# Attention in front of two dense layers: where a tile's values stand, who transposes the last tile, and how much filling a late step gets

## The chip, the cores and the metric

One core of a Trainium2 chip runs the kernel. The metric is device time in microseconds (us); lower is better. PE is TensorE, DVE VectorE, ACT ScalarE, POOL GpSimd, and SP the engine whose queue issues most DMAs.

## The reference

Batch 2, 8 heads, 768 positions, head dimension 64. Each position attends to the first 8 positions and to the last 96, with a bias that falls with distance; then two dense layers follow, a mixture of four experts and a SoLU layer.

```python
scores = scale * np.matmul(q, k.transpose(0, 1, 3, 2)) + bias
scores = np.where(keep, scores, -1e9)
a = softmax(scores)
attn = np.matmul(a, v)                       # x: 1536 tokens of 512
for e in range(E):                           # 4 experts, hidden 1024
    out += p[:, e:e + 1] * (np.maximum(x @ w1[e], 0.0) @ w2[e])
h = out @ w_in                               # SoLU layer, LayerNorm, then
return layernorm(h * softmax(h)) * g_ln @ w_out
```

## The kernel before, in words

The 1536 queries stand in 12 tiles of 128. A unit is one tile and one pair of heads, so unit u belongs to tile u // 4, and there are 48. The first 14 units are worked one by one. From then on the loop at line 1571 takes steps t = 14, 16, ..., 50 and starts two units in each. A pair of units passes through these stages, each in a later step:

- Step t: `scores` (L1223), two PE products per unit into one PSUM tile, `sps`. In `soft_pair` DVE then adds the bias and finds the maximum (L1274), and ACT takes the exponential (L1281).
- Step t+2: `soft_pair` normalizes the pair (sum L1260, reciprocal L1261, product L1265 on POOL or DVE). Then the probabilities are transposed, in one of two ways. The plain way is `stage_b`: eight PE transposes (L1305) and two ACT copies into `pts` (L1307). The other is `turn`: two DVE block transposes (L1317), a DMA store, and in step t+4 four DMA loads into `pts_turned` (`turned_back`, L1324). `turned(u)` says which it is: the first two units of the tiles in `TURNED`.
- The values, `stage_c` (L1350): sixteen PE products per pair into the PSUM tile `x`. A plain pair has them at the end of step t+4, a turned pair at the front of step t+8. After the last pair of a tile, ACT copies `x` into `xh` (L1363) and DVE subtracts the rest into `xl` (L1364). There is one `x` tile, so the next tile's first values need L1364 done. The turned pair of a tile is its last one.

Between these stages the loop calls `pull(share)`, twice in most steps. It issues pieces of the first expert's products, three PE matmuls each (L552 or L583, 256 wide for the first 512 tokens, 512 wide for the next), until their cost (320 or 640) has used up the share. An overrun or a rest is carried to the next pull. A pull also ends where the next block of tokens isn't ready, which drops the rest, and between the two products of a block of tokens 512 wide, which keeps it (`yield 0, None`, L848). What no pull has issued runs after the loop, in `rest_of_moe`; the last block of 512 tokens always does, since it needs all of attention.

The share of a step is 2 x 312, from step 36 on 2 x 750, plus half of (1970 - other), where `other` counts the step's transposes and values. The order of instructions on every engine is the order of the program (`manual_schedule`).

On the trace, step 24 begins with the scores at 55.84 us, step 26 at 61.89, step 32 at 76.14, 34 at 82.19, 36 at 86.26, 42 at 104.33, 44 at 111.33 and 46 at 117.99. Steps 48 and 50 have no scores: their first values begin at 124.35 and their last at 129.82, and the last block of the first expert starts at 132.32.

Of the kernel before, what the change touches and what calls it, by code (L numbers as in the profile page):

```python
# [34 lines left out]
EARLY = 312  # L35
# [11 lines left out]
HALF = 512  # L47
PAIRS = 14
FORMS = 36
TURNED = 4, 6, 8, 9, 10, 11  # L50


@with_exitstack
def kernel(ctx, tc, ep, qk, vp, nn, pr, wall, w64, gl, out):
# [1093 lines left out]
    def fast_arm():  # L1148
        st = stream("f")
        with ExitStack() as es:  # L1150
# [24 lines left out]
            st_p, st_rs, st_pt, st_x = {}, {}, {}, {}  # L1175
            NU = 4 * NSLOT
            NAT = 2
            N0 = 4 * NAT

            def unit(u):  # L1180

                return (u % 2, u // 2) if u < N0 else divmod(u, 4)
# [11 lines left out]
            def load_v(s):  # L1194
                if s < NSLOT:
                    v = vpl.tile([128, 2, 512], F32, tag="v", name="v")
                    nc.sync.dma_start(out=v, in_=vp[s])
                    vts[s] = v

            def geom(s):  # L1200

                if SLOTS[s][1] == 0:
                    return 1, None, (1,)
                if KEY_OF[s] % RING == 0:
                    return 2, 128, (1, 0)
                return 2, 0, (0, 1)

            def scores(u):

                s, pr_ = unit(u)  # L1210
                pos = KEY_OF[s] % RING
                out_ = sps[:, :, u % 2]
                for a in range(2):
                    r = slice(64 * a, 64 * a + 64)
                    if geom(s)[0] == 1:
                        nc.tensor.matmul(out_[:, a, 0:128], lhsT=qs[s][r, pr_], rhs=kr[r, pr_, pos, 32:160],
                                         start=True, stop=True)
                    else:

                        k = kr[r, pr_, 0, 0:128]  # L1220
                        c0, d = (32, 160 * (RING - 1) - 32) if pos == 0 else (160 * (pos - 1), 192)
                        rhs = bass.AP(tensor=k.tensor, offset=k.offset + c0, ap=[list(k.ap[0]), [d, 2], [1, 128]])
                        nc.tensor.matmul(out_[:, a], lhsT=qs[s][r, pr_], rhs=rhs, start=True, stop=True)  # L1223
# [86 lines left out]
            def turned(u):  # L1310

                return u % 4 < 2 and u // 4 in TURNED

            def turn(u0):
                for u in (u0, u0 + 1):
                    p, k = st_p.pop(u), 4 * (u % 2)
                    nc.vector.transpose(out=blocks.rearrange("p (jj c q) -> p c jj q", jj=4, c=8)[:, k:k + 4],  # L1317
                                        in_=p.rearrange("p a (c jj f) -> p (a c) jj f", c=2, jj=4))
                nc.sync.dma_start(out=t_dram[u0 // 4 % 2], in_=blocks)
# [10 lines left out]
            def stage_c(u, hold=None):  # L1330
                s, pr_ = unit(u)
                nch, _, parts = geom(s)
                t = st_pt.pop(u)
                if u < N0:
                    x, place = x0[:, 2 * (pr_ % 2):2 * (pr_ % 2) + 2], s
                else:
                    if s not in st_x:
                        st_x[s] = psX.tile([128, 4, 128], F32, tag="x", name="x")
                    x, place = st_x[s], pr_
                for c in range(nch):  # L1340
                    for a in range(2):
                        h = 2 * pr_ + a
                        if s < NAT:
                            v = v0[:, s, 64 * h:64 * h + 64]
                        else:
                            v = vts[s][:, parts[c], 64 * h:64 * h + 64]
                        to, r = x[64 * a:64 * a + 64, place], t[nch * a + c]
                        if turned(u):
                            to = to.rearrange("p (i q) -> p i q", i=4)
                        nc.tensor.matmul(to, lhsT=v, rhs=r,  # L1350
                                         start=(c == 0), stop=(c == nch - 1))
                if u < N0 and s == NAT - 1:
                    xc = slice(pr_, pr_ + 1), slice(0, 128 * NAT)
                elif u >= N0 and pr_ == (1 if turned(u) else 3) and not turned(u - 2):
                    xc = slice(0, 4), slice(128 * s, 128 * s + 128)
                else:
                    return
                h_, l_ = xh[:, xc[0], xc[1]], xl[:, xc[0], xc[1]]
                if u < N0:
                    x = x.rearrange("p s c -> p (s c)").unsqueeze(1)  # L1360

                def evict():
                    nc.scalar.copy(h_, x)  # L1363
                    late.append(lambda: nc.vector.tensor_tensor(out=l_, in0=x, in1=h_.bitcast(F32), op=ALU.subtract))  # L1364

                if hold is None:
                    evict()
                else:
                    hold.append(evict)
# [74 lines left out]
            def next_operands(s, pr_):  # L1444

                if pr_ == 0:
                    for j in LOAD_AFTER.get(s - 1, ()):
                        load_keys(j, copies)
                    if s > 3:
                        load_q(s + 1)  # L1450
# [70 lines left out]
            for t in range(N0, PAIRS):  # L1521
                s, pr_ = divmod(t, 4)
                share = SHARE.get(t, EARLY if t < N0 + 12 else 400 if t < N0 + 27 else 750)
# [46 lines left out]
                    st.load_piece()  # L1570
            for t in range(PAIRS, NU + 3, 2):

                other = 870 * (not turned(t - 2)) + 1100 * (not turned(t - 4)) + 1100 * turned(t - 8)
                share = 2 * (EARLY if t < N0 + 27 else 750) + (1970 - other) // 2
                hold, landed = [], copies[:]
                del copies[:]
                if t < NU:
                    for u in (t, t + 1):
                        scores(u)
                if turned(t - 8) and t <= NU:  # L1580
                    for u in (t - 8, t - 7):
                        stage_c(u, hold)
                if t < NU:
                    for u in (t, t + 1):
                        next_operands(*divmod(u, 4))
                if turned(t - 4):
                    turned_back(t - 4)
                if turned(t - 8):
                    load_v((t - 8) // 4 + 2)
                soft_pair(t)  # L1590
                for f in landed:
                    f()
                while late:
                    late.pop()()
                while st.rests:
                    st.rests.pop(0)()
                for f in hold:
                    f()
                if turned(t - 2):
                    turn(t - 2)  # L1600
                if t <= NU:
                    st.behind = False
                    pull(share)
                for _ in range(2):
                    next(rest_p, None)
                if t <= NU and not turned(t - 2):
                    for u in (t - 2, t - 1):
                        stage_b(u)
                if t < NU:
                    tokens[0] = 128 * done  # L1610
                    st.behind = t < NU - 2
                    if t > PAIRS:
                        pull(share)
                while late:
                    late.pop()()
                if not turned(t - 4):
                    for u in (t - 4, t - 3):
                        if u in st_pt:
                            stage_c(u)
                if t > NU and turned(t - 6):  # L1620
                    pull(share)
                    for u in (t - 6, t - 5):
                        stage_c(u)
                if t % 4 == 2 and not turned(t - 6):
                    done = (t - 2) // 4
                    load_v(done + 1)
                elif turned(t - 8):
                    done = (t - 4) // 4
                if t == FORMS:
                    st.forms = st.x_forms(lambda: [st.rawp.tile([128, 512], F32, tag="raw", name="fraw")  # L1630
                                                   for k in range(2)])
                if st.forms and t < NU:
                    for f in st.forms.pop(0):
                        f()
                if t < NU:
                    for u in (t, t + 1):
                        st.split_piece("act" if u < N0 + 12 and u % 2 else "dve", "pool")
                        st.load_piece()
# [180 lines left out]
```

## Time and profile before

| What | Value |
|---|---|
| Median of 3 runs | 725.35 us (725.05 to 726.32) |
| Profiled execution | 723.35 us, its span 721.6 us |
| PE busy | 705.5 us, 98% of the span |
| DVE, POOL, ACT busy | 498.5, 350.6, 301.2 us |
| Chain that ended last | PE 92%, DVE 3%, ACT 2%, DMA 1%, issue 1% |
| Granted TensorE clock | 1.000 of full speed |

Busy shares are means over stages with different limits. A row of the timeline has the start, the duration, the engine, line and operation, and in brackets how long the engine had been idle and what released it. Ends of matmuls are modelled and overlap the next start, so the time that PE loses at a wait is read from starts to starts.

### The profile page before, as it was taken

To read this page: it belongs to the slowest core of one execution; us is meant where nothing else is said; L and a number is where in the kernel's file an instruction comes from. 1 tells how busy PE (TensorE), PEld (TensorE's weight loads), DVE (VectorE), ACT (ScalarE), POOL (GpSimd) and SP (SyncE) were. 2 spreads that over 40 slices of the span, in tenths; PEclk is the share of its full clock that TensorE was granted. 3 is DMA by queue.
4 is the path that set the end of the run, shared out by engine and by line. 5 is a ranking of instruction groups with operands and counts; after the bars stand their busy time and mean duration, and the time that the engine had idled before them with its cause. 6 is when DMAs were issued, how large, how long until landed. Compare 5 with 4: busy or idle time off the path is not lost.

```text
span 721.6 us, 11067 instructions
## 1 busy us (share of the span) xinstructions
PE 705.5 (98%) x3815; PEld 586.5 (81%) x3815; DVE 498.5 (69%) x1088; ACT 301.2 (42%) x676; POOL 350.6 (49%) x407
## 2 busy tenths in 40 slices
PE   8999899899999999999999999999999999999997
PEld 5787777688889889888888988888898888888886
DVE  6776656647785685677568568857965667778870
ACT  5876654422533333242333325324434324454452
POOL 6733476466694156218216522630735089555600
PEclk9999999999999999999999999999999999999999
DMA  8655563420342324234132423423332690333341
GB/s 252 149 170 160 155 175 118 146 74 15 118 134 86 102 89 117 62 101 131 59 107 84 132 73 110 123 69 97 99 103 73 249 362 1 120 115 124 111 129 50
DMA packets 59921, 85.61 MB, mean 119 GB/s; under 512 B 6224, under 2 KB 37200, under 8 KB 59856
## 3 DMA queue, kind: packets, MB, share of 16 engines
q1 hardware_dynamic: 59296, 84.39, 37.3%
q8 instruction: 32, 0.52, 0.3%
q10 hardware_dynamic: 560, 0.43, 0.2%
q14 instruction: 33, 0.27, 0.1%
HBM read 62.75 MB, written 22.04 MB: 118 GB/s over the span
## 4 chain that ended last, share of the span: by engine, by line
PE 92%; DVE 3%; ACT 2%; DMA 1%; issue 1%; SPq 0%; POOL 0%; DVEq 0%; POOLq 0%; ACTq 0%
PE fg L583 36%; PE fg L760 18%; PE fo L1088 9%; PE fh L989 8%; PE fg L675 7%; PE fg L552 5%; PE x L1350 3%; PE sps L1223 3%; PE pt L1305 1%; PE g L1377 1%; PE wp L134 1%; DVE fg L688 1%; DVE p L1274 1%; DMA v<-in_vp_dram 1%; ACT fhh L644 1%
## 5 line engine op out<-in xcount | busy, mean ns | idle before, releaser
L583 PE MATMUL fg<-fhh,wV 128*128 128x512 f32 (+1 forms) x800 | 242.0, 383 | 0.3
L583 PEld LDWEIGHTS fg<-fhh,wV 128*128 128x128 f32 x800 | 147.9, 188 | 32.9 <-issue 2.5
L583 PE MATMUL fg<-fhl,wV 128*128 128x512 f32 (+1 forms) x400 | 149.2, 381 | 0.3 <-DVE fhl L567 0.2
L583 PEld LDWEIGHTS fg<-fhl,wV 128*128 128x128 f32 x400 | 74.9, 188 | 15.3 <-DVE fhl L567 0.8
L309 POOL TENSOR_TENSOR wR<-kr,wR 128x512 fp32r<-128x512 f32 (+1 forms) x28 | 29.1, 1060 | 96.4 <-ACT wR L301 96.3
L644 ACT ACTIVATE fhh<-fg 128x512 fp32r<-128x512 f32 x80 | 47.5, 598 | 66.6 <-DVE fg L770 40.3
L602 POOL TENSOR_TENSOR scr<-scr,kr 128x512 f32<-128x512 f32 x24 | 31.0, 1293 | 61.5 <-DVE kr L601 61.5
L645 DVE SCALAR_TENSOR_TENSOR fhl<-fg,fhh 128x512 fp32r<-128x512 f32 x80 | 54.1, 686 | 7.0 <-ACT fhh L644 5.4
L760 PE MATMUL fg<-xt,fwS 128*128 128x512 f32 x252 | 58.3, 389 | 0.0
L760 PEld LDWEIGHTS fg<-xt,fwS 128*128 128x128 f32 x252 | 47.3, 188 | 9.8
L760 PE MATMUL fg<-xh,wR 128*128 128x512 f32 x168 | 54.0, 389 | 0.0
L770 DVE TENSOR_TENSOR fg<-kr,fg 128x512 f32<-128x512 f32 x42 | 29.0, 694 | 33.4 <-PE fg L760 23.0
L597 DVE TENSOR_TENSOR fg<-fg,pb 128x512 f32<-128x512 f32 x59 | 40.9, 693 | 14.6 <-PE fg L583 14.2
L1265 POOL TENSOR_TENSOR p<-p,su 128x512 f32<-128x512 f32 x24 | 28.0, 1179 | 45.3 <-DVE su L1261 30.9
L1281 ACT ACTIVATE p<-p,mn 128x256 f32<-128x256 f32 x68 | 33.9, 499 | 28.8 <-DVE mn L1274 27.7
L598 DVE TENSOR_TENSOR scr<-fg,scr 128x512 f32<-128x512 f32 x59 | 40.8, 692 | 2.0
L552 PE MATMUL fg<-xh,wR 128*128 128x512 f32 (+1 forms) x128 | 38.6, 372 | 1.4 <-DVE xl L1364 1.4
L760 PEld LDWEIGHTS fg<-xh,wR 128*128 128x128 f32 x168 | 31.5, 188 | 6.6
L309 POOL TENSOR_TENSOR fwS<-kr,fwS 128x512 fp32r<-128x512 f32 x28 | 35.8, 1299 | 2.2 <-ACT fwS L301 2.2
L1274 DVE CUSTOM_DVE_ANT_0 p<-sps,btab 128x256 f32<-128x256 f32 x68 | 25.0, 420 | 15.7 <-PE sps L1223 15.6
L1088 PE MATMUL fo<-xt,fhh 128*128 128x512 f32 (+1 forms) x156 | 35.4, 375 | 0.0
L765 ACT COPY kr<-fg 128x512 f32<-128x512 f32 x42 | 24.2, 590 | 25.6 <-PE fg L760 25.6
(286 smaller groups left out, 1501.7 us busy)
## 6 DMA issues: line engine op xcount, KB each, us to landing
w_dram<-fr SPq DMA_DIRECT2D x44, 256.0 KB, 2.5
kr<-in_wall_dram SPq DMA_DIRECT2D x42, 256.0 KB, 2.9
fr<-in_w_dram SPq DMA_DIRECT2D x32, 256.0 KB, 2.7
pb<-p_dram SPq DMA_DIRECT2D x22, 256.0 KB, 3.3
v<-in_vp_dram SPq DMA_DIRECT2D x10, 512.0 KB, 4.0
kr<-t_dram SPq DMA_DIRECT2D x32, 128.0 KB, 2.9
frawt<-in_wall_dram SPq DMA_DIRECT2D x14, 256.0 KB, 2.8
t_dram<-tmp SPq DMA_DIRECT2D x6, 512.0 KB, 3.0
```

Of the source, the lines that this page charges most:

```text
L309: e.tensor_tensor(out=w[:, 1], in0=t, in1=w[:, 0].bitcast(F32), op=ALU.subtract)
L552: nc.tensor.matmul(ps[:, :n], lhsT=w[:, a, k], rhs=b[:, k, cols], start=(k == 0 and i == 0), stop=(k == 3 and i == 2))
L583: nc.tensor.matmul(ps[:, :n], lhsT=w[:, a, k], rhs=b[k], start=(i == 0), stop=(i == 11))
L597: nc.vector.tensor_tensor(out=ps[:, :n], in0=ps[:, :n], in1=pg, op=ALU.mult)
L598: nc.vector.tensor_tensor(out=a, in0=ps[:, :n], in1=a, op=ALU.add)
L644: nc.scalar.activation(th, src, AF.Relu)
L645: residuals.append(lambda: nc.vector.scalar_tensor_tensor(out=tl, in0=src, scalar=0.0, in1=th.bitcast(F32), op0=ALU.max, op1=ALU.subtract))
L675: nc.tensor.matmul(ps[:, q_ * q:q_ * q + q_], lhsT=w[:, a, j], rhs=x[b][j], start=(opens and q == j == m == 0), stop=(j == 1 and m == 2), ...
L760: nc.tensor.matmul(ps, lhsT=w[:, a, j], rhs=x[b][j], start=(i in (1, 2, 5) and j == 0 and m == 0), stop=(j == 1 and m == 2), skip_group_ch ...
L989: nc.tensor.matmul(ps[i], lhsT=left[i][x][j], rhs=right[i][j][:, y], start=(i in (1, 5, 2) and j == m == 0), stop=(j == 1 and m == 2), ski ...
L1088: nc.tensor.matmul(ps, lhsT=a[:, fc % 4], rhs=wo[fc][:, i % 2, c0:c0 + n], start=(fc == i == 0), stop=(fc == 7 and i == 2))
L1281: nc.scalar.activation(p[:, a], p[:, a], AF.Exp, bias=mn[:, a:a + 1], scale=-1.0, accum_out=st_rs[u][:, a, 0:1])
```

## The change

The last tile, 11, is no longer turned. Where the tile before has a turned pair, the values of the next tile's first two units move from step t+4 to step t+6, where they stand together with those of its last two units. The share from step 36 on is 2 x 680 in place of 2 x 750, and `other` counts the values of a step as they now stand.

```diff
-TURNED = 4, 6, 8, 9, 10, 11
+TURNED = 4, 6, 8, 9, 10
+LATE = 680
...
+            def valued(t):
+
+                if turned(t - 4) or turned(t - 8) and t <= NU:
+                    return []
+                return list(range(t - 6 if turned(t - 10) and not turned(t - 6) else t - 4, t - 2))
...
-                other = 870 * (not turned(t - 2)) + 1100 * (not turned(t - 4)) + 1100 * turned(t - 8)
-                share = 2 * (EARLY if t < N0 + 27 else 750) + (1970 - other) // 2
+                other = 870 * (not turned(t - 2)) + 550 * len(valued(t)) + 1100 * turned(t - 8)
+                share = 2 * (EARLY if t < N0 + 27 else LATE) + (1970 - other) // 2
...
-                if not turned(t - 4):
-                    for u in (t - 4, t - 3):
-                        if u in st_pt:
-                            stage_c(u)
+                for u in valued(t):
+                    if u in st_pt:
+                        stage_c(u)
```

`valued` gives no units in steps 24 and 32 and four in steps 26 and 34; it gives units 44 to 47 in step 50. The branch for a turned pair at the end (`if t > NU and turned(t - 6)`), which had one more pull in step 50, is no longer taken.

## Rows read from the trace of the kernel before

**Rows 1.** part 1 of the page: busy time, share and instructions by engine.

```profile
PE 705.5 (98%) x3815; PEld 586.5 (81%) x3815; DVE 498.5 (69%) x1088; ACT 301.2 (42%) x676; POOL 350.6 (49%) x407
```

**Rows 2.** stretches: busy us (instructions) of PE, PEld, DVE, ACT, POOL; clock; DMA.

```profile
118.00:124.40 6.40, 6.40 (x45) 4.96 (x46) 6.11 (x20) 2.59 (x9) 4.62 (x4) 1.00 0.21 85
124.40:132.30 7.90, 4.97 (x63) 3.92 (x57) 3.57 (x6) 3.00 (x6) 0.41 (x1) 1.00 0.73 218
132.30:721.60 589.30, 583.97 (x2840) 493.12 (x2840) 410.30 (x736) 219.16 (x411) 280.88 (x324) 1.00 0.33 106
```

**Rows 3.** waits of PE from 30 to 135 us: total us, times, longest us.

```profile
PE x L1350 <- DVE xl L1364: 2.4, 2, 1.4
PE x L1350 <- DMA pts_turned<-t_dram: 1.4, 2, 1.0
PE fg L552 <- DVE xl L1364: 1.4, 1, 1.4
PE x L1350 <- ACT pts L1307: 0.6, 1, 0.6
```

**Rows 4.** timeline of PE, steps 24 and 26.

```profile
59.28 0.36 PE L552 MATMUL fg<-xh,wR 128*128 128x256 f32 x1
...
60.87 1.09 PE L1350 MATMUL x<-pts,v 128*64 128x128 f32 x16 [0.99 <-DVE xl L1364]
61.89 1.14 PE L1223 MATMUL sps<-kr,q 64*128 64x256 f32 x8
```

**Rows 5.** timeline of PE, steps 32 to 36.

```profile
78.69 1.03 PE L1305 MATMUL pt<-ident,p 128*128 128x128 f32 x8
81.17 1.09 PE L1350 MATMUL x<-pts,v 128*64 128x128 f32 x16 [1.45 <-DVE xl L1364]
82.19 1.14 PE L1223 MATMUL sps<-kr,q 64*128 64x256 f32 x8
83.26 0.39 PE L583 MATMUL fg<-fhh,wV 128*128 128x256 f32 x1
...
85.23 1.09 PE L1350 MATMUL x<-pts,v 128*64 128x128 f32 x16
...
87.87 0.63 PE L1305 MATMUL pt<-ident,p 128*128 128x128 f32 x4 [0.48 <-DVE p L1265]
88.68 0.66 PE L1305 MATMUL pt<-ident,p 128*128 128x128 f32 x4 [0.18 <-POOL p L1265]
```

**Rows 6.** timeline of PE, steps 44 and 46.

```profile
115.62 1.03 PE L1305 MATMUL pt<-ident,p 128*128 128x128 f32 x8
116.41 0.48 PE L583 MATMUL fg<-fhh,wV 128*128 128x512 f32 x1
...
117.99 1.14 PE L1223 MATMUL sps<-kr,q 64*128 64x256 f32 x8
```

**Rows 7.** timeline of PE, steps 48 and 50 and the block behind them.

```profile
126.14 1.04 PE L1305 MATMUL pt<-ident,p 128*128 128x128 f32 x8
127.73 1.09 PE L1350 MATMUL x<-pts,v 128*64 128x128 f32 x16 [0.55 <-ACT pts L1307]
129.82 1.09 PE L1350 MATMUL x<-pts_turned,v 128*64 128x128 f32 x16 [0.99 <-DMA pts_turned<-t_dram]
132.32 0.50 PE L552 MATMUL fg<-xh,wR 128*128 128x512 f32 x1 [1.41 <-DVE xl L1364]
```

**Rows 8.** timeline of DVE, steps 32, 34 and 48.

```profile
80.42 0.69 DVE L1364 TENSOR_TENSOR xl<-x,xh 128x512 fp32r<-128x512 f32 x1 [1.64 <-ACT xh L1363]
...
84.78 1.30 DVE L1317 STREAM_TRANSPOSE tmp<-p 128x512 f32<-128x512 f32 x2
...
126.95 0.68 DVE L1364 TENSOR_TENSOR xl<-x,xh 128x512 fp32r<-128x512 f32 x1
```

**Rows 9.** timeline of POOL, the normalizing products of steps 34 and 46.

```profile
81.56 2.04 POOL L1265 TENSOR_TENSOR p<-p,su 128x512 f32<-128x512 f32 x2 [4.21 <-DVE su L1261]
...
119.71 2.04 POOL L1265 TENSOR_TENSOR p<-p,su 128x512 f32<-128x512 f32 x2 [3.61 <-DVE su L1261]
```

## The prediction

> **What bounds the kernel now.** I read part 1 of the page first: PE is busy for 98% of the span [rows 1], so time can come only from the places where PE stands still or from work taken off PE. The stretches come next. Behind 132.30 us PE is busy for 583.97 of 589.30 us, while just before it 4.97 of 7.90 us are busy [rows 2]. The part behind 132.30 can therefore only be shifted as a whole: what attention gains in front of it reaches the end, and what it loses does too. Then the waits of PE inside attention: 2.4 us in two waits of the values for L1364, 1.4 us in two for the loads of the turned pairs, 1.4 us at the first product behind attention, 0.6 us for the copies of the transposes [rows 3]. The timeline of PE shows where they lie: step 24, step 32, and four places in steps 48 and 50 seen as three gaps [rows 4, 5, 7].
>
> Because the ends of matmuls are modelled, I measure each gap from starts to starts. Prices first. A piece of filling 256 wide: five of them run from 83.26 to 85.23, 0.39 us each [rows 5]. A run of two pieces 512 wide: 116.41 to 117.99, 1.58 us; eight PE transposes: 115.62 to 116.41, 0.79 us [rows 6]. Sixteen value products: 60.87 to 61.89, 1.02 us [rows 4]. Scores of a step: 82.19 to 83.26, 1.07 us [rows 5].
>
> **Part one: values stand together a step later.** In step 24 PE ends its one piece at 59.28 + 0.39 = 59.67 and starts the values at 60.87, so 1.20 us are lost [rows 4]. In step 32 the transposes end at 78.69 + 0.79 = 79.48 and the values start at 81.17: 1.69 us [rows 5]. Both gaps have one cause. The turned pair at the front of the step completes its tile, and the next tile's values need the single `x` tile, which DVE's L1364 gives back at 80.42 + 0.69 = 81.11 [rows 8], behind ACT's exponentials and copy. The change puts these values behind the next step's scores and filling, some 3 us later, when L1364 is long done. The work itself is kept: adding up shares and costs, steps 24 and 26 issue 1 + 6 pieces now and 4 + 3 then, steps 32 and 34 1 + 5 and 4 + 2.
>
> What is late next is the pair's chain through DVE and POOL. The next wait, at the transposes of step 36 (87.87 and 88.68), stays, since there PE already runs ahead of L1265 [rows 5]. But that chain starts from the scores of step 34, which move 1.69 us earlier, so the wait moves with it if nothing in between is tied to something that doesn't move. One thing is: POOL's products of step 34 follow DVE's sum behind L1364, and run from 81.56 to 83.60 whatever PE does [rows 9]. DVE's two block transposes read them, the first from 84.78 - 1.6 = 83.2, the second some 0.65 later at 83.85 [rows 8]. The second product is done 0.25 us before; the cover is thin. If it is gone, the cost is what POOL is late by; from below the cost is 0, from above the gain of this step, 1.69 us. I take 0. Part one: 1.20 + 1.69 = 2.89 us.
>
> **Part two: the last tile is transposed by PE.** It adds eight transposes, 0.79 us of PE [rows 6], and two ACT copies. ACT has 2.59 us of work in the 6.40 us of step 46 [rows 2], which covers them. It removes two block transposes on DVE, one store and four loads. In steps 48 and 50 the gaps of PE are: from 126.14 + 0.79 = 126.93 to 127.73, 0.80 us for the copies of pair 46; from 127.73 + 1.02 = 128.75 to 129.82, 1.07 us for the loads of pair 44; from 129.82 + 1.02 = 130.84 to 132.32, 1.48 us for the eviction of the last tile [rows 7]. Together 3.35 us. The second goes, as there are no loads. The first goes too: the values of pair 44, transposed two steps before, now stand ahead of those of pair 46, and 0.79 + 1.02 = 1.81 us pass from the start of the transposes to the values of 46, where 127.73 - 126.14 = 1.59 us were needed [rows 7]. Pair 44 needs L1364 of the tile before; it ends at 127.63 now, held by a piece in front of it in DVE's order [rows 8], and 1.5 us more filling stands ahead of the transposes then.
>
> A new wait can come in step 46, at the transposes of pair 44, which need POOL's products. In the old order these end at 119.71 + 2.04 = 121.75 [rows 9]; PE would be there at 117.99 + 1.07 for scores + 1.58 for two pieces = 120.64, so the wait lies between 0 and 1.1 us. I take 0: the sum in front of the products was late because DVE's queue waited for the fourth piece of a group in the second pull of step 44, and with the new shares that group ends in the first.
>
> The Trainium skill ("VectorE: DVE Perf Modes", section on the three transpose paths) gives 390 ns for a 128x128 transpose on TensorE and 311 ns for VectorE's blocks. By its price the eight would cost an estimated 3.12 us in place of 0.79 and the whole gain would be about 3.0 us; the trace has them starting 0.1 us apart, and I hold to the trace.
>
> **Part three: smaller late shares.** They remove no work; they keep some for later. Added up from step 36 on, in pieces 512 wide: now 4, 6, 4, 6, 5, 6, 1, all 32 of the block, so nothing is left when the last tile is evicted. Then 3, 6, 4, 3, 7, 4, 3 = 30: two pieces are left, and no pull stands in step 50. They run behind the last values and before the last block, 1.58 us against the gap of 1.48 [rows 6, 7], so the third gap is covered. The second pull of step 42 issues nothing, as it meets the border between the two products; its credit goes to step 44. Step 42 is then short, 1.07 + three pieces + 1.02 us, some 4.3 us in all.
>
> **The sum.** 2.89 + 3.35 - 0.79 = 5.45 us; I take 5.3 for joints of 0.1 us. The profiled execution took 723.35 us, its span 721.6, and would come to 718.05. The median of the runs is 725.35, 2.0 us above the profiled one; I carry the same difference over: 725.35 - 5.3 = 720.1 us.
>
> **Rivals.**
> 1. The chain of one pair takes over: the waits of steps 24 and 32 go, but PE meets them again in step 36, since POOL's products of step 34 don't move [rows 9]. Against it: 0.25 us of cover. Gain 5.3 - 1.7 = 3.6 us, or 721.8 us.
> 2. The end doesn't pay: a new wait in step 46 (1.1 us) and two pieces that come too early or too late to cover the eviction (1.5 us). For it: the two pieces cross from one section of the program to the next, where buffers are laid out anew. Gain 5.3 - 2.6 = 2.7 us, or 722.7 us.
> 3. The change doesn't do what it says: the waits return at other places for nearly their whole length, because the steps run at the rate of DVE and POOL. Gain under 1.4 us, 724 to 726.8 us.
> 4. Slower: with fewer pieces in steps 36 to 46, PE falls to the rate of the chain from scores over DVE, ACT and POOL to the transposes, in each of six steps. DVE was busy for 6.11 of 6.40 us in step 46 [rows 2], which speaks for it; the two block transposes taken out there and the even filling of the other steps speak against. It decides from 5.3 / 6 = 0.9 us a step; at 1.2 us it costs 7.2 and gives 725.35 + 1.9 = 727.3 us.
>
> **How the numbers follow.** Forecast 0.58, rivals 0.15, 0.13, 0.08 and 0.06. Less than 0.2%, 1.45 us, can't be told from no change here. Faster by more: 0.58 + 0.15 + 0.13 = 0.86; same 0.08; slower 0.06. The range: at best the gaps go and the shorter runs of filling save some start costs, 6.7 us, 718.6; on the other side it takes in the first two rivals and the edge of the third, 723.9.
>
> **What would show it.** Right: no wait of L1350 for L1364; pair 20 and 28 behind the filling of steps 26 and 34; 136 transposes at L1305 and 80 value products from `pts_turned`; six L583 products between the last values and the first L552 of the last block, which starts without a wait; PE still waiting at the transposes of step 36 by about as much as now. Wrong: a wait of more than 0.5 us at L1305 in step 46, at L1223 in step 44, or a longer one in step 36; or idle time behind the last block's start, where I expect none new.

## The result: 7.65 us faster, where 5.3 were forecast

| | before | changed |
|---|---|---|
| Median of 4 runs | 725.84 us (725.05 to 726.98) | 718.19 us (717.23 to 718.84) |
| Profiled execution | 723.35 us, span 721.6 | 718.38 us, span 716.6 |
| Ratio | | 0.9892 (0.9874 to 0.9911) |

The forecast was 720.1 us in a range of 718.6 to 723.9. The measured 718.19 lies below it. The profiled execution, on the other hand, came to 718.38 where 718.05 was forecast. So what the forecast got wrong isn't in the difference of the two profiles; it is in what the runs of before have on top of their profile. The two profiles agree with the forecast in part by luck, as the end of this section shows.

First part 1 of the changed kernel's page (busy time, share of the span, instructions by engine), which answers to [rows 1]: PE is busy about as long as before, in a span that is 5.0 us shorter.

```profile
PE 706.1 (99%) x3823; PEld 587.7 (82%) x3823; DVE 497.8 (69%) x1086; ACT 302.1 (42%) x678; POOL 349.2 (49%) x407
```

Its waits of PE from 30 to 135 us (total, times, longest) answer to [rows 3]. L1357 is the old L1350, L1371 the old L1364, L1306 the old L1305. None of the waits for L1371 is left, neither of the values nor of the last block. One wait for a turned pair's loads remains.

```profile
PE x L1357 <- DMA pts_turned<-t_dram: 0.5, 1, 0.5
PE pt L1306 <- DVE mn L1275: 0.4, 1, 0.4
PE pt L1306 <- DVE p L1266: 0.3, 1, 0.3
PE pt L1306 <- POOL p L1266: 0.2, 1, 0.2
```

Its timeline of PE in steps 24 and 26 answers to [rows 4]: the scores of step 24 and the values of the turned pair, two pieces, the transposes, two pieces, the scores of step 26, and behind three more pieces 32 value products at once. No row has an idle time.

```profile
56.40 1.13 PE L1224 MATMUL sps<-kr,q 64*128 64x256 f32 x8
...
58.49 0.38 PE L553 MATMUL fg<-xh,wR 128*128 128x256 f32 x1
...
59.30 1.03 PE L1306 MATMUL pt<-ident,p 128*128 128x128 f32 x8
60.09 0.36 PE L553 MATMUL fg<-xh,wR 128*128 128x256 f32 x1
...
60.98 1.13 PE L1224 MATMUL sps<-kr,q 64*128 64x256 f32 x8
...
63.31 1.97 PE L1357 MATMUL x<-pts,v 128*64 128x128 f32 x32
```

Steps 32 to 36, for [rows 5]: the wait for the loads in step 32, the values of both pairs together, and the next wait, which stands where it stood, at the transposes of step 36, and came forward with everything else.

```profile
76.70 1.09 PE L1357 MATMUL x<-pts_turned,v 128*64 128x128 f32 x16 [0.50 <-DMA pts_turned<-t_dram]
...
82.19 1.97 PE L1357 MATMUL x<-pts,v 128*64 128x128 f32 x32
84.09 1.13 PE L1224 MATMUL sps<-kr,q 64*128 64x256 f32 x8
85.55 0.63 PE L1306 MATMUL pt<-ident,p 128*128 128x128 f32 x4 [0.33 <-DVE p L1266]
86.36 0.66 PE L1306 MATMUL pt<-ident,p 128*128 128x128 f32 x4 [0.18 <-POOL p L1266]
```

Steps 46 to 50, for [rows 6, 7]: the new transposes at 116.29, the last ones at 122.73, all values of the last tile at 123.69, two pieces at 125.59, and the last block at 127.07 without a wait. The two pieces are just enough: DVE's L1371, which that block needs, ends at 126.33 + 0.69 = 127.02.

```profile
116.29 1.03 PE L1306 MATMUL pt<-ident,p 128*128 128x128 f32 x8
...
122.73 1.04 PE L1306 MATMUL pt<-ident,p 128*128 128x128 f32 x8
123.69 1.97 PE L1357 MATMUL x<-pts,v 128*64 128x128 f32 x32
125.59 0.50 PE L584 MATMUL fg<-fhh,wV 128*128 128x512 f32 x1
...
127.07 0.50 PE L553 MATMUL fg<-xh,wR 128*128 128x512 f32 x1
```

```profile
126.33 0.69 DVE L1371 TENSOR_TENSOR xl<-x,xh 128x512 fp32r<-128x512 f32 x1 [3.51 <-ACT xh L1370]
```

From the scores of step 24 to the last block, PE takes 127.07 - 56.40 = 70.67 us, where it took 132.32 - 55.84 = 76.48 [rows 7]: 5.81 us less. What lies behind is no shorter, as the stretch that answers to [rows 2] shows (busy time of PE, weight loads, DVE, ACT, POOL; clock; DMA).

```profile
127.00:716.60 589.60, 584.19 (x2842) 493.09 (x2840) 411.44 (x738) 219.05 (x411) 280.24 (x324) 1.00 0.33 108
```

The spans differ by 5.0 us and not by 5.81, because step 24 begins 0.56 us later in this execution (56.40 for 55.84) and the part behind takes 0.3 us more. Nothing ahead of step 24 was changed; in the fourteen profiles of this case it begins anywhere from 55.80 to 57.08 us. So the forecast of 718.05 for the profiled execution came out within 0.33 us because a larger gain than the one summed up, 5.81 us for 5.45, came together with a later start.

### The profile page after: what moved, and what is told of

It reads as the page before. It is cut to its first block, busy times and chain, and to the rows that moved or that the text cites. A ratio compares the mean times of both kernels' runs of the same rounds, so it can differ in the third digit from the quotient of the medians.

```text
span 716.6 us, 11078 instructions
## 1 busy us (share of the span) xinstructions
PE 706.1 (99%) x3823; PEld 587.7 (82%) x3823; DVE 497.8 (69%) x1086; ACT 302.1 (42%) x678; POOL 349.2 (49%) x407
## 4 chain that ended last, share of the span: by engine, by line
PE 95%; DVE 1%; ACT 1%; SPq 1%; DMA 1%; issue 0%; POOL 0%; DVEq 0%
PE fg L584 37%; PE fg L761 19%; PE fo L1089 9%; PE fh L990 8%; PE fg L676 7%; PE fg L553 6%; PE x L1357 3%; PE sps L1224 2%; PE pt L1306 2%; PE g L1384 1%; PE wp L135 1%; DMA pts_turned<-t_dram 1%; DVE fg L689 1%; ACT fhh L645 1%; PE fh L1070 0%
```

## Experiments

The question was where the missing 2.35 us come from. Theory C: PE's gaps in steps 48 and 50 let the granted clock fall in most executions of the kernel before, though not in the profiled one. Rival S: the runs spread by chance at the start. The first four kernels also take the change apart.

**The kernel before against itself.**

> The kernel before, unchanged, timed against itself. The prediction carried the 2.0 us by which the runs of before lay above its profiled execution over to the changed kernel; there the profiled execution (718.38 us) lies among the runs (717.23 to 718.84). Theory S (start): the difference is chance at the start, where the granted clock rises at a time that varies; then this kernel's runs spread over 723 to 727 us at a granted clock of 0.998 to 1.000, and the profile loses or gains the time in the first 8 us. Rival C (clock behind the gaps): PE's gaps in steps 48 and 50 let the granted clock fall in some executions; then the runs at 725 to 727 us show 0.996 to 0.998, with the loss between 126 and 140 us, and a kernel without the gaps doesn't have them.

725.76 us, ratio 1.0006 (0.9991 to 1.0022). Its own profile has full clock throughout, but the runs, each listed with its mean granted clock, fall into groups. The 101 runs of the kernel before that were timed with these experiments:

| Mean granted clock | Runs | Median | Range |
|---|---|---|---|
| 0.999 and 1.000 | 25 | 723.57 us | 723.08 to 724.71 |
| 0.997 and 0.998 | 52 | 725.45 us | 723.16 to 726.16 |
| 0.996 and less | 24 | 726.84 us | 726.20 to 729.54 |

Where the clock is granted throughout, the kernel before takes about what its two profiles took, 723.35 and 723.52 us. About two runs in three lie above 724.7, nearly all with a lower mean clock. The size fits as well: a mean of 0.997 to 0.998 over 722 us is an estimated 1.4 to 2.2 us of lost clock, and the median of that group lies 1.9 us above the first. That fits C, but it doesn't show the place yet, and no profile of the kernel before caught a fall.

S is right about a smaller part. The first twelve products of PE take 4.38 to 5.49 us in the fourteen profiles, and the start of step 24 moves by 1.3 us; the 25 runs at full clock spread over 1.6 us.

**Part one alone** (`TURNED` with tile 11, `LATE = 750`).

```diff
-TURNED = 4, 6, 8, 9, 10
-LATE = 680
+TURNED = 4, 6, 8, 9, 10, 11
+LATE = 750
```

> Part one alone: the values behind a turned tile stand together a step later; the last tile stays turned and the late share stays 750. By the theory of the gaps PE loses 1.20 and 1.69 us less in steps 24 and 32 and the three gaps in steps 48 and 50 (3.35 us) stay: 2.9 us less than before, both in the runs and between the start of step 24 and the last block. By the rival that the chain through POOL takes the second gap back in step 36: 1.2 us. By C the runs stay above the profiled execution as those of before do.

721.60 us, ratio 0.9957 (0.9941 to 0.9972), 3.1 us less than before by that ratio. The four fastest runs, at full clock, lie at 720.57 to 720.80, 2.9 us under 723.5, as worked out; five of the twelve runs lie at 722.28 to 725.34, with 0.998 and less. This profile caught the clock falling. The rows are stretches of 2 us at the end of attention; the third column from the right is the granted clock (1.00 is 2.4 GHz, 0.50 is 1.2 GHz).

```profile
124.00:126.00 2.00, 1.45 (x14) 1.14 (x14) 1.30 (x3) 1.16 (x3) 0.00 (x0) 1.00 0.61 178
126.00:128.00 2.00, 1.02 (x18) 0.78 (x16) 0.00 (x0) 0.00 (x0) 0.00 (x0) 1.00 0.97 277
128.00:130.00 2.00, 0.96 (x16) 0.71 (x15) 0.38 (x1) 0.99 (x2) 0.00 (x0) 1.00 0.99 283
130.00:132.00 2.00, 1.63 (x5) 1.33 (x6) 2.00 (x4) 1.15 (x3) 0.94 (x1) 0.72 1.01 340
132.00:134.00 2.00, 2.00 (x7) 1.52 (x6) 2.00 (x2) 0.00 (x0) 1.92 (x2) 0.50 0.68 239
134.00:136.00 2.00, 2.00 (x10) 1.62 (x9) 1.86 (x2) 0.62 (x1) 1.37 (x2) 0.92 0.01 3
```

PE is busy for 1.45, 1.02 and 0.96 us of three stretches of 2 us; then, with PE busy again, the clock goes to half, and it is back in the last stretch. The part behind the start of the last block takes 720.9 - 130.37 = 590.5 us, 1.2 more than [rows 2]: that is about what this fall costs. The timeline of PE shows the same three gaps as [rows 7], and behind them two products that take 1.05 us at 132.24, where two take 0.63 in the kernel before (132.89).

```profile
125.79 1.09 PE L1357 MATMUL x<-pts,v 128*64 128x128 f32 x16 [0.56 <-ACT pts L1308]
127.86 1.09 PE L1357 MATMUL x<-pts_turned,v 128*64 128x128 f32 x16 [0.98 <-DMA pts_turned<-t_dram]
130.37 0.50 PE L553 MATMUL fg<-xh,wR 128*128 128x512 f32 x1 [1.41 <-DVE xl L1371]
...
132.24 1.05 PE L553 MATMUL fg<-xh,wR 128*128 128x512 f32 x2
```

**Part two alone** (the kernel before, with `TURNED = 4, 6, 8, 9, 10`).

> Part two alone: the last tile is transposed by TensorE, values where they stood before, late share 750. The wait for the loads (1.07 us) goes, eight transposes come (0.79 us), one piece of filling is left for the eviction (0.7 of 1.48 us). The values of units 44 and 45 now stand in step 48, behind those that complete the tile before, so by the theory of the gaps they wait for L1364 as in steps 24 and 32, 1.2 to 1.7 us: together 0.3 us faster to 0.7 us slower than before. By the rival that the loads were the costly part of the end: 2 us faster or more.

722.57 us, ratio 0.9958 (0.9943 to 0.9973), and all ten runs within 721.80 to 722.92 at a clock of 0.998 and above. From step 24 to the last block it takes 75.06 us, 1.4 less than before. Against the runs of before at full clock the median is 1.0 us lower; the rest of the 2.9 us below 725.47 is the clock of the runs of before, as no run of this kernel stands apart. My expectation was off: the values of pair 44 didn't wait for L1364, as a piece of filling and the transposes of pair 46 stand ahead of them; the timeline has all 32 value products right behind the transposes, and only the last wait is left, shortened.

```profile
127.17 1.04 PE L1305 MATMUL pt<-ident,p 128*128 128x128 f32 x8
128.14 1.97 PE L1350 MATMUL x<-pts,v 128*64 128x128 f32 x32
...
131.52 0.50 PE L552 MATMUL fg<-xh,wR 128*128 128x512 f32 x1 [0.52 <-DVE xl L1364]
```

**The changed kernel with late shares of 750** (`LATE = 750`).

> The changed kernel with late shares of 750 in place of 680: all 32 pieces of the block are issued before the last values, none is left behind them. By the theory of the gaps the first product of the last block waits again for the eviction, 1.4 to 1.5 us, and the kernel is that much slower than the changed one: 4.3 us less than before between step 24 and the last block. By the rival that the shares do nothing: as the changed one, 5.8 us less there.

720.82 us, ratio 0.9944 (0.9928 to 0.9961), 2.6 us more than the changed kernel and not 1.4 to 1.5. From step 24 to the last block it takes 128.96 - 56.05 = 72.91 us, 3.6 less than before and not 4.3. The gap ahead of the last block is back, and one of 0.79 us ahead of the last values with it. The profile names the transposes as the releaser, but they had long been done: the values need L1371 of the tile before, which ran until 125.48, held up in DVE's order by L589, which needed the piece that PE ends at 124.00. With shares of 680 the piece for L589 ends earlier, L1371 is done at 122.82, and the values don't wait. So the first gap of part two goes only where no piece holds up L1371. Two of the ten runs stand apart, at 722.58 and 723.78 us (0.998 and 0.992).

```profile
124.00 1.03 PE L1306 MATMUL pt<-ident,p 128*128 128x128 f32 x8
124.80 0.68 DVE L1371 TENSOR_TENSOR xl<-x,xh 128x512 fp32r<-128x512 f32 x1
125.58 1.97 PE L1357 MATMUL x<-pts,v 128*64 128x128 f32 x32 [0.55 <-PE pt L1306]
128.96 0.50 PE L553 MATMUL fg<-xh,wR 128*128 128x512 f32 x1 [1.40 <-DVE xl L1371]
```

**Idle matmuls in the gaps of the kernel before.** Now the clock by itself: the waits stay, but PE works during them.

```diff
+            def busy(n):
+                for _ in range(n):
+                    nc.tensor.matmul(idle, lhsT=xh[:, 0, 0:128], rhs=xh[:, 0, 0:512], start=True, stop=True)
...
+                if t > NU:
+                    idle = st.psp.tile([128, 512], F32, tag="g", name="idle")
+                    busy(3)
                 if not turned(t - 4):
...
                 if t > NU and turned(t - 6):
                     pull(share)
+                    busy(4)
...
+            busy(6)
             tokens[0] = NT
```

> The kernel before, with idle matmuls (their result is not used) in the three gaps of steps 48 and 50: 3, 4 and 6 of 0.23 us each ahead of the values of pair 46, of pair 44 and of the last block. No wait is taken away. By theory C (the granted clock falls behind the gaps in some executions, which costs them 2 to 4 us) the runs at 725.5 us and above are gone and all lie near 723.5: median 1.9 us below before at no change of the fastest run. By theory S (the spread comes from the start) the runs stay spread over 723 to 727.5 with the same median.

724.06 us, ratio 0.9978 (0.9962 to 0.9994). All twelve runs lie at 723.38 to 724.69 and 0.998 to 1.000; of the kernel before, timed beside it, 24 of 29 lay above 724.8. Useless work made the kernel 1.4 us faster at the median and no faster at its best. That decides for C, and leaves S only the spread of 1.3 us among these twelve: the place is the end of attention, and what PE does in the gaps is the cause. The idle matmuls cost something too (77.25 us from step 24 to the last block in place of 76.48), which goes the way of the 1.4 us where 1.9 were expected.

**Only the last gap filled** (`busy(0)`, `busy(0)`, `busy(6)`).

> The kernel before, with idle matmuls in the last gap alone (6 of 0.23 us ahead of the last block); the gaps of 0.80 and 1.07 us stay. By C the share of slow runs falls with the idle time that is left: 1.9 of 3.35 us idle, as in the changed kernel with late shares of 750, whose runs were slow 2 times in 10: median 723.5 to 724.3. By S: 725.5, as before.

724.14 us, ratio 0.9990 (0.9977 to 1.0004), so by the interval it can't be told from before; but only three of twelve runs are at 0.992 to 0.996 and 725.25 to 727.20. The profile is one that fell: stretches of 2 us as above. Two gaps were enough for it, the second of them longer than in [rows 7], as the loads came later (1.49 us of idle time for 0.99). The clock is already down in the stretch from 130 us, and the matmuls of the last gap, from 132.02 on, run at half clock.

```profile
130.38 1.72 PE L1350 MATMUL x<-pts_turned,v 128*64 128x128 f32 x16 [1.49 <-DMA pts_turned<-t_dram]
```

```profile
128.00:130.00 2.00, 0.89 (x16) 0.65 (x12) 0.00 (x0) 0.00 (x0) 0.00 (x0) 1.00 1.03 261
130.00:132.00 2.00, 1.62 (x16) 1.32 (x16) 0.00 (x0) 0.00 (x0) 0.00 (x0) 0.67 1.06 303
132.00:134.00 2.00, 2.00 (x7) 1.61 (x6) 1.25 (x3) 1.87 (x4) 0.00 (x0) 0.50 1.02 369
```

**Only the first two gaps filled** (`busy(3)`, `busy(4)`, `busy(0)`).

> The kernel before, with idle matmuls in the gaps ahead of the values of pairs 46 and 44 (3 and 4 of 0.23 us); the gap of 1.48 us ahead of the last block stays. By C 1.5 of 3.35 us idle are left, and few runs or none are slow: median 723.5 to 724. By S: 725.5, as before.

723.82 us, ratio 0.9982 (0.9971 to 0.9993), all twelve runs at 0.998 and above. With the last gap alone, of 1.4 us, no run stands apart.

**The changed kernel made to stand still.** The reverse: its gaps are gone, so put one back.

```diff
+                if t > NU:
+                    for k in range(5):
+                        nc.vector.tensor_copy(out=tmp2[:, (k + 1) % 2], in_=tmp2[:, k % 2])
+                    hold_up = psT.tile([128, 4, 128], F32, tag="pt", name="pt")
+                    nc.tensor.transpose(hold_up[:, 0], tmp2[:, 1, 0:128], ident)
                 for u in valued(t):
```

> The changed kernel, with PE made to stand still in step 50: one transpose of scratch data waits for five DVE copies of 128x512 (about 3 us) ahead of the last values. By the theory of the gaps alone it is slower than the changed kernel by the length of the stillness, 2.5 to 3 us, 721 us, with all runs near each other. By C some runs show a granted clock of 0.992 to 0.997 with half speed behind the last values and cost 2 to 4 us more: median 722.5 to 724, and the runs apart in two groups.

720.49 us, all six runs at 0.999 and above, and no second group. The stillness came out shorter than meant, as a copy takes 0.45 us:

```profile
125.74 0.30 PE L1627 MATMUL pt<-ident,tmp 128*128 128x128 f32 x1 [1.39 <-DVE tmp L1625]
```

So this kernel says no more than the one before it: behind a single gap of 1.4 us none of 18 runs is below 0.998. With 13 copies:

> The changed kernel with PE made to stand still longer in step 50: 13 DVE copies in place of 5. Five stood it still for 1.4 us and cost 2.3 us, with no fall of the clock; 13 take 3.6 us more, so about 5 us of stillness. By the gaps alone: 720.5 + 3.6 = 724.1 us in all runs at a clock of 0.999 and above. By theory C the clock now falls behind it in most runs, for 2 to 4 us more: median 726 to 728, clock 0.992 to 0.997.

725.68 us, ratio to before 1.0005 (0.9992 to 1.0018). Every one of twelve runs is at 0.997 or less, and the median is 1.6 us above what the stillness explains (724.1), though below the 726 to 728 that I expected. The timeline of PE and the stretches around it:

```profile
128.09 0.40 PE L1627 MATMUL pt<-ident,tmp 128*128 128x128 f32 x1 [5.08 <-DVE tmp L1625]
128.42 3.48 PE L1357 MATMUL x<-pts,v 128*64 128x128 f32 x32
```

```profile
126.00:128.00 2.00, 0.00 (x0) 0.00 (x0) 1.80 (x5) 0.00 (x0) 0.00 (x0) 1.00 0.00 0
128.00:130.00 2.00, 1.91 (x17) 1.72 (x19) 0.00 (x0) 0.00 (x0) 0.00 (x0) 0.54 0.04 8
130.00:132.00 2.00, 2.00 (x21) 1.83 (x18) 0.00 (x0) 0.05 (x1) 0.00 (x0) 0.61 0.00 0
132.00:134.00 2.00, 2.00 (x9) 1.48 (x10) 1.16 (x2) 2.00 (x4) 0.00 (x0) 1.00 0.00 0
```

Right behind 5.1 us of idle time the 32 value products take 3.48 us where they take 1.97 in the changed kernel. That is 1.5 us, nearly all of the 1.6 that the fall costs here.

**Part three alone** (`680` for `750` in the kernel before).

> Part three alone: late shares of 680, nothing else changed. Three pieces that before stood in steps 36 to 46 then stand in steps 48 and 50, two ahead of the transposes of pair 46 and one ahead of the values of pair 44, where PE waited for the loads (1.07 us); none is left for the last block, whose gap of 1.48 us stays. By the theory of the gaps 0.7 us less than before, and by theory C, as less idle time stands together, fewer slow runs: median 723.2. By the rival that the shares do nothing without the other parts: 725.4.

722.48 us, ratio 0.9964 (0.9947 to 0.9980), all ten runs at 0.998 and above, 1.1 us under the runs of before at full clock; 74.90 us from step 24 to the last block, 1.6 less than before and not 0.7. The rows, beside [rows 7], show where: the piece ahead of pair 44's values hides their loads, and the wait ahead of pair 46's values is 0.29 us and no longer 0.55. The wait of 0.23 us for L567, in step 42 of the kernel before, is gone too.

```profile
126.32 1.14 PE L1350 MATMUL x<-pts,v 128*64 128x128 f32 x16 [0.29 <-ACT pts L1307]
...
128.30 1.09 PE L1350 MATMUL x<-pts_turned,v 128*64 128x128 f32 x16
130.80 0.50 PE L552 MATMUL fg<-xh,wR 128*128 128x512 f32 x1 [1.41 <-DVE xl L1364]
```

**A step beyond.** The wait that is left in step 32 is for loads; in step 28 one key load now follows them.

```diff
-                    for j in LOAD_AFTER.get(s - 1, ()):
+                    for j in LOAD_AFTER.get(s - 1, ())[:1]:
                         load_keys(j, copies)
...
                     turned_back(t - 4)
+                if t % 4 == 0 and t < NU:
+                    for j in LOAD_AFTER.get(t // 4 - 1, ())[1:]:
+                        load_keys(j, copies)
```

> A step beyond the changed kernel: in step 28 the second of two key loads is issued behind the loads of the turned pair in place of ahead of them, since the values of that pair wait 0.50 us for these loads in step 32. By the theory of the gaps the wait goes: 0.5 us below the changed kernel, 717.7 us, which the profile shows better than the times. Rival: the pair's chain through DVE and POOL takes it back in step 36: as the changed one, 718.2.

The wait in step 32 is gone from the profile, and a wait of 0.33 us for the loads in step 24 is there, which the changed kernel has in one of its two profiles and not in the other. The best run is 717.39 us, the median of six 718.18: no gain that can be told from the changed kernel. Two of the six stand at 721.13 and 721.53 us with 0.991 and 0.992.

**The changed kernel once more.**

> The changed kernel, unchanged, once more, to have as many of its runs as of the others. By theory C it has no gaps behind which the clock falls: runs of 717 to 719 us, median 718.2, and at most one in ten at a clock under 0.997. Against it: with one key load issued later, otherwise the same, 2 of 6 runs stood at 721.1 and 721.5 us and 0.991 to 0.992; if the changed kernel shows such runs as often, something beside the gaps of steps 48 and 50 lets the clock fall too, and C explains only a part.

718.42 us, ratio 0.9911 (0.9897 to 0.9925), five runs from 718.08 to 718.64 at 0.998 and above. With the first four that makes nine runs of the changed kernel, none at less than 0.998 and none above 718.84. Nine runs are few: falls in one run of five would go unseen in nine with a chance of 0.13. What let the clock fall in two runs with the key load moved isn't shown: its profile is of a run that didn't have it. That stays open.

## Why the prediction was wrong, step by step

**The step that failed** is "I carry the same difference over". The 2.0 us between the profiled execution of before and the median of its runs were taken for a fixed offset. They are what half clock costs behind the gaps of steps 48 and 50, in the two runs of three in which it falls; the profiled execution was one of the others. The change removes these gaps, so the difference goes too: the runs of the changed kernel lie 0.2 us below its profiled execution, and not 2.0 above. That the gaps are the cause is shown by filling them, which took the runs with a lower clock away; that it is half clock is read from the falls in the profiles of other kernels, since neither profile of before has one. Like against like, the runs of before at full clock have a median of 723.57 us and the nine runs of the changed kernel 718.39: 5.2 us, against a forecast of 5.3. The rest of the 7.65 us is the clock, with 0.5 us of chance in it: the median of before stood at 725.35 with three runs and at 725.84 with the fourth. The range ended at a gain of 6.7 us, built from the gaps and some start costs that no row showed, and couldn't hold it. A hint was there: the runs of before spread over 1.3 us around a median 2.0 us above the profile, and I named no reason for it.

With 13 copies the clock fell behind one idle time of 5.1 us, in 12 runs of 12. The Trainium skill ("TensorE: Matmul & The Clock Gate", part 1) says that an idle TensorE goes to 1.2 GHz; these runs agree. With part one alone it fell in some runs behind three gaps of 0.8 to 1.5 us with values in between. The Trainium skill (the same page, the section on a second failure mode) tells of another kernel in which short idles between groups of matmuls made the clock swing between its two levels; the stretches above agree.

**Part one.** Right in its gaps: both went, 2.7 us from step 24 to step 36 (30.42 to 27.69 us) where 2.89 were summed up. The wait in step 36 is 0.33 + 0.18 us modelled, 0.48 + 0.18 before [rows 5]. Rival 1 is out. The thin cover of 0.25 us wasn't put to the test. POOL's products end at 80.50 + 2.04 = 82.54, and the second block transpose starts some 0.65 us behind 82.79, so 0.9 us lie between.

```profile
80.50 2.04 POOL L1266 TENSOR_TENSOR p<-p,su 128x512 f32<-128x512 f32 x2 [4.22 <-DVE su L1262]
```

```profile
82.79 1.30 DVE L1324 STREAM_TRANSPOSE tmp<-p 128x512 f32<-128x512 f32 x2
```

The prediction let step 34 come 1.69 us nearer to step 32; it came 0.88 us nearer (5.17 us from scores to scores for 6.05), because the pair of step 32 waits 0.50 us for its loads and step 32 has more pieces in it. I hadn't seen that such a wait stood in the kernel before too, hidden in front of the one for L1364. Its second profile shows it: 0.68 us for the loads, and 0.71 for L1364 where [rows 5] have 1.45, with the values at the same 81.17.

```profile
77.94 1.09 PE L1350 MATMUL x<-pts_turned,v 128*64 128x128 f32 x16 [0.68 <-DMA pts_turned<-t_dram]
...
81.17 1.09 PE L1350 MATMUL x<-pts,v 128*64 128x128 f32 x16 [0.71 <-DVE xl L1364]
```

Without the wait for L1364 the loads' wait counts. In part one alone those of steps 24 and 32 took 1.45 us together, which is why its profile shows only 1.9 us between step 24 and the last block.

**Part two.** Right: all three gaps of the end are gone, 136 transposes and 80 products from `pts_turned` are there as forecast, the eight added transposes cost 0.79 us (116.29 to 117.08), no loads are waited for, and PE doesn't wait in step 46. POOL's products end 1.1 us before the transposes read them:

```profile
113.19 2.04 POOL L1266 TENSOR_TENSOR p<-p,su 128x512 f32<-128x512 f32 x2 [1.01 <-ACT pts L1308]
```

Rival 2 is out. The Trainium skill ("VectorE: DVE Perf Modes", section on the three transpose paths) gives 390 ns for a transpose on TensorE, and that is not the price of each one here: the eight start 0.1 us apart in the changed kernel too.

**Part three.** Right in what it does: two pieces of filling are left, and the last block starts behind them without a wait. Mis-sized when taken alone: 1.6 us and not 0.7, in the main by waits that I had put down to part two. The parts overlap; from step 36 to the last block the whole change brings 3.08 us (46.06 to 42.98), where 2.56 were summed up. The difference is two waits that the sum left out: the one for L567 in the kernel before, some 0.4 us from starts to starts, which is gone, and the one in step 36, which is 0.15 us shorter.

```profile
109.66 0.50 PE L583 MATMUL fg<-fhl,wV 128*128 128x512 f32 x1 [0.23 <-DVE fhl L567]
```

**Rivals 3 and 4.** Out: no wait appeared in steps 38 to 46, and the short step 42 didn't stop PE.

## What to carry to other kernels

Ask of a wait on PE not only how long it is but what other waits stand near it: here three gaps of 0.8 to 1.5 us close together cost their 3.35 us and, in two runs of three, another 2 us or more of half clock behind them. When the median of the runs lies above the profiled execution by more than the runs spread, look for the reason before carrying the difference over: list the runs with their granted clock and see whether they form groups. Idle matmuls in the gaps tell the clock's share from the wait's share without taking a wait away.

## What wasn't expected of the hardware

With part one alone the granted clock fell to half without one long stillness before it: PE had been busy for 1.45, 1.02 and 0.96 us of the three stretches of 2 us ahead, and 1.63 us of the one in which it fell. Whether it falls differs from run to run of one kernel, and the length of the gaps doesn't decide it alone: the wait for the last loads was 0.98 us in that profile, and 1.24 us in the second profile of the kernel before, which kept its clock. With the last gap filled 3 of 12 runs are at 0.996 or less. And a fall at the very end costs nothing: the changed kernel's profile shows 0.50 from 714 us on, behind its last product at 711.12, and its span is 716.6 us, as in its second profile, which has a mean of 1.000. That is why a mean of 0.998 alone doesn't tell a run that lost time.
